# Reordering the start of a fused convolution, SoLU and layer-norm kernel on one Trainium2 core

## The chip, the core and the metric

One core of one Trainium2 chip runs the whole kernel. The engines are TensorE (PE, matmuls; PEld are its weight loads), VectorE (DVE), ScalarE (ACT), GpSimd (POOL) and SyncE (SP), which issues the transfers. The metric is device time in microseconds of one execution, the median of the runs shown. A profile is one further execution; its own clock starts at its first event.

## The reference

`x` is 8 x 4160 x 192. Each of 8 heads (24 columns) has a causal filter of 7 taps, the softmax of its row of `weight`; the result is a matrix of 33,280 rows and 192 columns. Then a layer of 1,024 features:

```python
h = x @ w_in                                  # 192 -> 1024
e = np.exp(h - h_max)                         # h_max: maximum of the row
sm = e / (np.sum(e, axis=-1, keepdims=True) + 1e-09)
solu = h * sm
mu = np.mean(solu, axis=-1, keepdims=True)
var = np.mean((solu - mu) ** 2, axis=-1, keepdims=True)
ln = (solu - mu) / np.sqrt(var + 1e-06) * g_ln
return (ln @ w_out).astype(np.float32)        # 1024 -> 192
```

`w_in` and `w_out` arrive as 64-bit floats, which the kernel reads as pairs of 32-bit words. All matmuls with weights are done in 16-bit halves: a tensor is scaled by a power of two and split into an upper part (rounded to fp16) and a lower part (what is left).

## The kernel before, in words

Rows are worked in 260 tiles of 128. A chunk of x (`xr`) gives its convolution as matmuls with the taps (`pc`, in chunk 0 `pq` and `pr`), split into uppers and lowers in `y`; transposing transfers turn y into `yT`. For a tile, ten matmuls form the scores `ph` (128x1024) from `yT` and `whi`/`wlo`; VectorE takes the maximum (`emit_max`, L803), ScalarE the exponential and its sum (`emit_exp`, L810), VectorE the product of scores and exponentials with its sum (`emit_mul`, L820). ScalarE casts that to the upper part of `p` (`emit_hi`, L831) and GpSimd forms the remainder (`emit_lo`, L846); transposed, they are multiplied with w_out (`po`, L878). There are three score buffers: tile 3 takes tile 0's, the convolution of the next chunk tile 1's, tile 4 tile 2's, each after that tile's product (`emit_mul`).

The order of instructions on each engine is the order of the code; nothing reorders it. Before the steady loop the kernel prepares what all tiles need. The places that the change touches:

- `root_power` (L100 to L113): from a sum of squares a power of two, in four VectorE steps on 128x1 that work on the bits. It gives `s` (scale of chunk 0 of x, from `c0.scale_steps`, L192), `t_in` (w_in, L635) and `t_out` (w_out, L697).
- `sum_squares` (L174): partial sums of squares of x on ScalarE, added up by a matmul (`pt_x`).
- The class `Words` (from L436) rebuilds a weight from its two words: `exponents` (L456) and `mantissas` (L461) mask the high word on VectorE, `lows` scales the low word on GpSimd (L467), `floats` turns the mantissa into a float on ScalarE (L473), `whole` adds both on GpSimd (L484), `join` does the last three at once on VectorE (L490), `powers` forms the power of two on ScalarE (L496), `signs` adds the sign on VectorE (L499), `value` multiplies mantissa and power (L506), `squares` sums the squares on ScalarE (L479). w_in goes through in three parts of 128x512 (`halves[0]`, `halves[1]`, `Z`), w_out at once, 128x1536 (`e_out`, `m_out`, `raw_out`, `f_out`).
- With `t_in`, ScalarE writes the uppers `whi` (L638, L650) and VectorE the lowers `wlo` (L653). `cv` holds the factors for the scores.
- w_out's powers are multiplied by g (`gl`) in `out_powers` (eight ScalarE steps, L692), and summed as squares. GpSimd multiplies the mantissas by them (`value`), `out_mean` (L708) takes column means by matmul, and `out_upper`, `out_lower` (L717 to L726) write the halves `ohl`, with `t_out`.
- `first_two` (L1169) and `second_two` (L1196) issue the steps of tiles 0 to 3 among all this.

Loads of the next chunks of x and of g, and the transposes of y, are issued on SP's queue in the order of the code.

## Time and profile before

| | us |
|---|---|
| median of 3 runs | 1154.21 (1152.86 to 1156.37) |
| span of the profiled execution | 1151.2 |
| of it TensorE busy | 1131.2 (98%) |
| VectorE, ScalarE, GpSimd busy | 994.3, 989.2, 891.5 |
| first score matmul of tile 0 | begins at 17.7 |
| first output matmul | begins at 43.1 |

The span runs from the first to the last event of one execution, which has no time of its own beside it. Times below are microseconds from the span's start, so that 43.1 is the point in the program at which the first output is formed. TensorE's granted clock is a share of full speed, 2.4 GHz. A line number belongs to the kernel that the sentence speaks of.

### The profile page before, as it was taken

The numbers are of one execution on the slowest core, as the hardware profiler recorded it, in microseconds if no ns is written. First come the engines' busy times: TensorE is split into PE (matmuls) and PEld (weight loads), VectorE is DVE, ScalarE is ACT, GpSimd is POOL, SyncE is SP. The second block draws the span as 40 slices with busy tenths as digits, with TensorE's granted clock in tenths as the row PEclk, the third lists the DMA queues.
The fourth block names the chain that finished last, engine by engine and source line by source line (L and its number), as shares of the span: only waits on it lengthen the run. The fifth ranks groups of instructions, "written<-read, shape, count | busy, mean of one in ns | idle before, by whom it ended". The sixth has DMA issues, their size and how long they took to land.

```text
span 1151.2 us, 22389 instructions
## 1 busy us (share of the span) xinstructions
PE 1131.2 (98%) x7742; PEld 691.9 (60%) x7742; DVE 994.3 (86%) x2024; ACT 989.2 (86%) x1789; POOL 891.5 (77%) x709
## 2 busy tenths in 40 slices
PE   5999999999999999999999999999999999999998
PEld 3675656665666666656666566666656666566556
DVE  8888898988888898888888888888888887888787
ACT  7888998888888888988889898888888889888885
POOL 3866899978788687888868788687888868855664
PEclk9999999999999999999999999999999999999999
DMA  7999999999999999999999999999999998999987
GB/s 227 186 184 185 202 207 209 214 206 211 201 213 198 195 204 198 216 191 213 197 204 190 207 199 203 196 205 206 193 213 200 193 205 160 178 164 189 187 158 179
DMA packets 727423, 226.95 MB, mean 197 GB/s; under 512 B 651646, under 2 KB 725902, under 8 KB 727310
## 3 DMA queue, kind: packets, MB, share of 16 engines
q1 hardware_dynamic: 727310, 225.53, 101.9%
q8 instruction: 60, 0.98, 0.3%
q14 instruction: 53, 0.43, 0.1%
HBM read 33.00 MB, written 25.56 MB: 51 GB/s over the span
## 4 chain that ended last, share of the span: by engine, by line
PE 86%; POOL 4%; ACT 3%; issue 2%; DVE 2%; DMA 2%; SPq 1%; POOLq 0%; ACTq 0%; DVEq 0%
PE po L878 39%; PE ph L743 35%; PE pc L281 6%; PE ph L772 5%; POOL p L846 2%; ACT sq L835 1%; DMA pT<-p 1%; DMA raw_in<-in_moe_w_in_dram 1%; DVE ph L803 1%; ACT e L810 1%; POOL xs L243 1%; DMA yT<-y 1%; DVE e L820 0%; POOL xr L240 0%; ACT xs L234 0%
## 5 line engine op out<-in xcount | busy, mean ns | idle before, releaser
L846 POOL TENSOR_TENSOR p<-e,p 128x1024 f16<-128x1024 f32 x257 | 547.6, 2135 | 190.1 <-ACT p L831 189.2
L878 PE MATMUL po<-ohl,pT 128*128 128x192 f16 (+1 forms) x4264 | 539.6, 284 | 0.5
L878 PEld LDWEIGHTS <-pT 128*128 128x128 f16 x4264 | 384.4, 98 | 159.7 <-issue 1.7
L743 PE MATMUL ph<-whi,yT 128*128 128x512 f16 x1548 | 419.4, 380 | 1.7 <-DVE e L820 1.5
L803 DVE TENSOR_SCALAR_CACHE_REDUCE ph<-ph,cv 128x1024 f32<-128x1024 f32 x248 | 319.4, 1289 | 88.4 <-PE ph L772 70.2
L810 ACT ACTIVATE e<-ph,sm 128x1024 f32<-128x1024 f32 x260 | 289.1, 1112 | 100.4 <-DVE ph L803 92.9
L820 DVE SCALAR_TENSOR_TENSOR e<-ph,cv,e 128x1024 f32<-128x1024 f32 x248 | 317.1, 1279 | 24.5 <-ACT e L810 24.1
L743 PEld LDWEIGHTS <-yT 128*128 128x128 f16 x2064 | 192.3, 98 | 230.1 <-issue 36.3
L831 ACT CAST p<-e 128x1024 f16<-128x1024 f32 x245 | 254.4, 1039 | 25.7 <-DVE e L820 23.2
L835 ACT ACTIVATE sq<-e 128x1024 f32<-128x1024 f32 x260 | 273.2, 1051 | 0.2
L743 PE MATMUL ph<-wlo,yT 128*128 128x512 f16 x516 | 153.6, 379 | 0.0
L888 DVE TENSOR_REDUCE raw<-po 128x192 f32<-128x384 f32 x247 | 136.9, 554 | 15.5 <-PE po L878 15.1
L243 POOL TENSOR_TENSOR xs<-xr,xs 128x960 f16<-128x960 f32 (+1 forms) x56 | 107.5, 1919 | 1.3
L772 PE MATMUL ph<-wlo,yT 64*128 64x512 f16 x269 | 74.4, 380 | 0.7 <-DVE e L820 0.7
L281 PE MATMUL pc<-xs,taps_hi 128*112 128x240 f16 (+1 forms) x448 | 72.9, 261 | 0.0
L322 DVE SCALAR_TENSOR_TENSOR y<-pc,y 112x432 f16<-112x432 f32 (+5 forms) x140 | 72.3, 533 | 0.5 <-ACT y L313 0.4
L313 ACT ACTIVATE y<-pc 112x432 f16<-112x432 f32 (+5 forms) x140 | 62.6, 468 | 11.2 <-PE pc L281 5.3
L772 PE MATMUL ph<-wlo,y 64*128 64x512 f16 x251 | 69.0, 380 | 0.0
L181 DVE TENSOR_REDUCE xa<-xr 128x1 f32<-128x384 f32 x112 | 66.7, 618 | 0.0
L281 PEld LDWEIGHTS <-taps_hi 128*112 128x112 f16 x448 | 52.4, 130 | 16.0
L240 POOL TENSOR_SCALAR xr<-xr,s 128x960 f32<-128x960 f32 (+1 forms) x56 | 57.4, 1025 | 3.3 <-ACT xs L234 0.4
L281 PE MATMUL pc<-xs,taps_lo 128*112 128x240 f16 (+1 forms) x224 | 58.5, 261 | 0.0
(150 smaller groups left out, 781.7 us busy)
## 6 DMA issues: line engine op xcount, KB each, us to landing
out_dram<-raw SPq DMA_DIRECT2D x127, 192.0 KB, 2.9
xr<-in_x_dram SPq DMA_DIRECT2D x41, 480.0 KB, 4.9
xr<-in_x_dram SPq DMA_DIRECT2D x22, 384.0 KB, 4.2
pT<-p SPq DMA_TRANSPOSE x263, 4.6
y<-yT SPq DMA_DIRECT2D x15, 140.0 KB, 3.0
y<-yT SPq DMA_DIRECT2D x15, 126.0 KB, 2.7
yT<-y SPq DMA_TRANSPOSE x102, 3.6
raw_out<-in_moe_w_out_dram SPq DMA_DIRECT2D x1, 1536.0 KB, 10.3
```

Of the source, the lines that this page charges most:

```text
L243: (2.1 * size + 0.2, lambda: pool.tensor_tensor(xl, r, h, ALU.subtract)),
L281: nc.tensor.matmul(o, tp[:, h + j, :], r, start=q == 0, stop=q == len(ops) - 1)
L743: nc.tensor.matmul(bank, lhs, w[:, r, n * 512 : (n + 1) * 512], start=start and j == 0, stop=stop and j == len(ops) - 1,)
L772: nc.tensor.matmul(banks_of(t)[n], y[q, t.off : t.off + P], wlo[q, 1, n * 512 : (n + 1) * 512], start=start, stop=not start,)
L803: dve.tensor_scalar(t.ph, t.ph, t.cv[:, 0:1], None, ALU.mult, ALU.min, accum_out=t.bias)
L810: act.activation(t.e, t.ph, AF.Exp, bias=t.bias, scale=-1.0, accum_out=grp.z[:, g : g + 1])
L820: dve.scalar_tensor_tensor(t.e, t.ph, t.cv[:, 3:4], t.e, ALU.mult, ALU.mult, accum_out=t.grp.s1[:, t.g : t.g + 1],)
L831: act.copy(t.p16[:, :, 0, :], t.halves)
L835: act.activation(junk, t.e, AF.Square, accum_out=t.grp.s2[:, t.g : t.g + 1])
L846: eng.tensor_tensor(t.p16[:, :, 1, :], t.halves, t.p16[:, :, 0, :], ALU.subtract)
L878: nc.tensor.matmul(t.po[:, 0:n], t.pT[:, a, :], w, start=j == 0, stop=j == len(ops) - 1)
L888: dve.tensor_reduce(t.grp.raw[:, t.g, :], t.po[:, 0 : 2 * D].rearrange("p (a d) -> p d a", a=2), AX.X, ALU.add,)
```

## The change

1. `root_bits` takes the place of `root_power` for the first `s`, for `t_in` and in `out_scale`: a multiply and a power of -1/2 on GpSimd, then one mask on VectorE (`t_out`'s multiply stays on VectorE).
2. The last 128x576 sum of squares of chunk 0 is done on VectorE; the matmul that adds up the sums comes after all but the last of the first convolution's matmuls.
3. The uppers and lowers of y's first three pieces are written between the steps of w_in's parts; w_in's third part starts later in VectorE's order.
4. g is loaded right behind w_out's words.
5. g is multiplied into w_out's lows (GpSimd, eight steps) and floats (ScalarE, eight steps); `out_powers` is gone.
6. Two of the last four uppers of w_in are written by GpSimd (`upper_twin`).
7. w_out's masks stand ahead of the last lowers of w_in; its signs behind tile 0's product; its powers ahead of tile 0's exponential; the last pieces of y behind tile 1's product.
8. The squares of w_out are summed from the finished floats `f_out` (`out_squares`), behind tile 3's exponential.

```diff
+    def root_bits(dst, src, num, tiny):
+        bits = dst.bitcast(I32)
+        return [
+            lambda: pool.tensor_scalar(dst, src, tiny, 1.0 / num, ALU.max, ALU.mult),
+            lambda: pool.tensor_tensor(dst, dst, mhalf, ALU.pow),
+            lambda: dve.tensor_scalar(bits, bits, EXPO, None, ALU.bitwise_and),
+        ]
...
+            if vector:
+                junk = sp.tile([P, F], F32, name=f"xv_{self.ch}_{col}", tag="e", bufs=4)
+                r = self.raw[j][:, a:z, :]
+                dve.scalar_tensor_tensor(
+                    junk[:, 0 : (z - a) * D].rearrange("p (w d) -> p w d", d=D),
+                    r, 1.0, r, ALU.mult, ALU.mult, accum_out=self.part[:, col : col + 1],
+                )
+                return
...
+    nc.sync.dma_start(gl, g_ln.rearrange("(c p) -> p c", p=P))
...
-        def lows(self, c, scale):
+        def lows(self, c, scale, by):
...
-        def floats(self, c):
-            act.copy(self.m[:, c].bitcast(F32), self.m[:, c])
+        def floats(self, c, by):
+            act.activation(
+                self.m[:, c].bitcast(F32), self.m[:, c], AF.Copy, scale=by
+            )
...
+    def upper_twin(to, of, q):
+        pool.tensor_scalar(to, of, t_in[q], 1.0, ALU.mult, ALU.mult)
...
+    chain0[1]()
+    wi.mantissas(halves[1])
+    for f in chain0[2:4]:
+        f()
+    wi.join(halves[1])
+    chain0[4]()
+    wi.squares(halves[1], isq[:, 1:2])
+    steps[0][0]()
+    wi.signs(halves[1], wi.m)
+    wi.exponents(Z)
+    wi.powers(Z)
+    wi.value(halves[1], wi.m, pool)
+    wi.mantissas(Z)
+    steps[1][0]()
+    wi.squares(Z, isq[:, 2:3])
+    wi.join(Z)
+    steps[2][0]()
+    steps[0][1]()
...
+    wi.signs(Z, wi.m)
+    dve.tensor_reduce(isq[:, 0:1], tp, AX.X, ALU.add)
+    settle_in = root_bits(t_in, isq[:, 0:1], 2.0**26, 1e-12)
+    for f in settle_in[:2]:
+        f()
+    steps[1][1]()
+    settle_in[2]()
...
+    upper_twin(whi[top, 1, 0:HF], wf[top, Z], top)
+    upper_in(whi[low, 1, 0:HF], wf[top, Z], top)
+    upper_twin(whi[low, 1, HF:F], wf[low, Z], low)
+    upper_in(whi[top, 1, HF:F], wf[low, Z], low)
+    wo.exponents(W)
+    wo.mantissas(W)
...
+    for j, c in enumerate(eighths):
+        wo.lows(c, 2.0**-32, gl[:, j : j + 1])
+    for j, c in enumerate(eighths):
+        wo.floats(c, gl[:, j : j + 1])
...
+    def out_squares():
+        junk = sp.tile([P, F], F32, name="oj_out", tag="sq", bufs=1)
+        act.activation(
+            junk.bitcast(F16)[:, 0 : NFC * D], wo.f, AF.Square, accum_out=osq
+        )
...
     first_two:
         emit_max(t)
+        wo.powers(W)
         emit_exp(t)
-        wo.mantissas(W)
-        wo.floats(W)
         wo.whole(W)
-        wo.signs(W, wo.e)
-        emit_mul(t)
-        out_powers()
         emit_max(u)
         emit_exp(u)
-        wo.squares(W, osq)
+        emit_mul(t)
+        wo.signs(W, wo.e)
+        emit_mul(u)
+        for pc, hg in got0:
+            c0.upper(pc, *hg)
         emit_hi(t)
         settle_rest()
-        emit_mul(u)
         emit_hi(u)
...
     second_two:
-        scale = out_scale()
         emit_max(t)
         emit_exp(t)
         out_mean()
         emit_max(u)
         emit_exp(u)
-        emit_square(tiles[0])
+        out_squares()
+        scale = out_scale()
         for f in scale:
             f()
+        emit_square(tiles[0])
         numerators(t)
```

The order on two engines, at three places. VectorE around w_in's third part (`e_in`, `m_in`, `f_in` are the exponent, mantissa and value; `xm` the sum of x, `isq` that of w_in), before:

```order
L456 TENSOR_SCALAR e_in<-raw_in 128x512
L461 TENSOR_SCALAR m_in<-raw_in 128x512
L203 TENSOR_REDUCE xm_170<-pt_x_178 128x1
L105 TENSOR_SCALAR s_171<-xm_170 128x1
L106 TENSOR_SCALAR s_171<-s_171 128x1
L109 TENSOR_SCALAR s_171<-s_171 128x1
L112 TENSOR_SCALAR s_171<-s_171 128x1
L499 SCALAR_TENSOR_TENSOR m_in<-raw_in,e_in 128x512
L490 SCALAR_TENSOR_TENSOR f_in<-raw_in,m_in 128x512
L634 TENSOR_REDUCE isq<-pt_wi 128x1
L105 TENSOR_SCALAR t_in<-isq 128x1
L106 TENSOR_SCALAR t_in<-t_in 128x1
```

and now:

```order
L514 SCALAR_TENSOR_TENSOR f_in<-raw_in,m_in 128x512
L121 TENSOR_SCALAR s_168<-s_168 128x1
L523 SCALAR_TENSOR_TENSOR m_in<-raw_in,e_in 128x512
L478 TENSOR_SCALAR e_in<-raw_in 128x512
L483 TENSOR_SCALAR m_in<-raw_in 128x512
L514 SCALAR_TENSOR_TENSOR f_in<-raw_in,m_in 128x512
L654 SCALAR_TENSOR_TENSOR y_0_0_191<-pq,s_168,y_0_0_191 112x5x96
L523 SCALAR_TENSOR_TENSOR m_in<-raw_in,e_in 128x512
L687 TENSOR_REDUCE isq<-pt_wi 128x1
L654 SCALAR_TENSOR_TENSOR y_0_0_191<-pq,s_168,y_0_0_191 112x5x32
L121 TENSOR_SCALAR t_in<-t_in 128x1
L654 SCALAR_TENSOR_TENSOR y_0_0_191<-pq,s_168,y_0_0_191 112x5x64
```

The masks of the third part (the last `e_in`, `m_in`) stood before the reduction to `xm`; they now stand behind `s` and the signs of the second part, and the pieces of y (`y_0_0`) between the steps up to `t_in`.

ScalarE from w_in's last uppers to tile 1's exponential and on (`e_298`, `e_315` before and `e_309`, `e_314` now are the exponentials of tiles 0 and 1), before:

```order
L650 ACTIVATE whi<-f_in,t_in 64x512 x4
L313 ACTIVATE y_0_0_198<-pr_207,s_171 112x5x96
L313 ACTIVATE y_0_0_198<-pr_208,s_171 112x5x32
L313 ACTIVATE y_0_0_198<-pr_208,s_171 112x5x64
L496 ACTIVATE e_out<-e_out,rebias 128x1536
L810 ACTIVATE e_298,z_269<-ph_274,sm_296 128x1024
L473 CAST m_out<-m_out 128x1536
L692 ACTIVATE e_out<-e_out,gl 128x192 x8
L810 ACTIVATE e_315,z_269<-ph_275,sm_313 128x1024
L479 ACTIVATE oj_out_317,osq<-e_out 128x1536
```

and now:

```order
L495 ACTIVATE m_out<-m_out,gl 128x192 x8
L520 ACTIVATE e_out<-e_out,rebias 128x1536
L870 ACTIVATE e_309,z_279<-ph_284,sm_306 128x1024
L870 ACTIVATE e_314,z_279<-ph_285,sm_312 128x1024
L333 ACTIVATE y_0_0_191<-pr_208,s_168 112x5x96
L333 ACTIVATE y_0_0_191<-pr_209,s_168 112x5x32
L333 ACTIVATE y_0_0_191<-pr_209,s_168 112x5x64
L891 CAST p_0_322<-e_309 128x2x512
L891 CAST p_1_331<-e_314 128x2x512
L870 ACTIVATE e_380,z_279<-ph_347,sm_378 128x1024
L870 ACTIVATE e_393,z_279<-ph_358,sm_391 128x1024
L745 ACTIVATE oj_out,osq<-f_out 128x1536
```

The cast of `m_out` and the eight multiplications of `e_out` by `gl` stood behind tile 0's exponential; eight steps on `m_out` and the powers of `e_out` now stand ahead of it, and the squares of w_out (`oj_out`) have left this stretch for the place behind tile 3's exponential.

VectorE from tile 0's maximum to tile 2's product (`e_298` and `e_380` before, `e_309` and `e_380` now), before:

```order
L803 TENSOR_SCALAR ph_274,sm_296<-ph_274,cv_172 128x1024
L461 TENSOR_SCALAR m_out<-raw_out 128x1536
L499 SCALAR_TENSOR_TENSOR e_out<-raw_out,e_out 128x1536
L820 SCALAR_TENSOR_TENSOR e_298,s_0_270<-ph_274,cv_172,e_298 128x1024
L803 TENSOR_SCALAR ph_275,sm_313<-ph_275,cv_172 128x1024
L322 SCALAR_TENSOR_TENSOR y_0_0_198<-pr_207,s_171,y_0_0_198 112x5x96
L322 SCALAR_TENSOR_TENSOR y_0_0_198<-pr_208,s_171,y_0_0_198 112x5x32
L322 SCALAR_TENSOR_TENSOR y_0_0_198<-pr_208,s_171,y_0_0_198 112x5x64
L820 SCALAR_TENSOR_TENSOR e_315,s_0_270<-ph_275,cv_172,e_315 128x1024
L803 TENSOR_SCALAR ph_345,sm_378<-ph_345,cv_172 128x1024
L803 TENSOR_SCALAR ph_356,sm_391<-ph_356,cv_172 128x1024
L105 TENSOR_SCALAR t_out<-pt_wo 128x1
```

and now, from tile 1's maximum:

```order
L863 TENSOR_SCALAR ph_285,sm_312<-ph_285,cv_169 128x1024
L880 SCALAR_TENSOR_TENSOR e_309,s_0_280<-ph_284,cv_169,e_309 128x1024
L523 SCALAR_TENSOR_TENSOR e_out<-raw_out,e_out 128x1536
L880 SCALAR_TENSOR_TENSOR e_314,s_0_280<-ph_285,cv_169,e_314 128x1024
L342 SCALAR_TENSOR_TENSOR y_0_0_191<-pr_208,s_168,y_0_0_191 112x5x96
L342 SCALAR_TENSOR_TENSOR y_0_0_191<-pr_209,s_168,y_0_0_191 112x5x32
L342 SCALAR_TENSOR_TENSOR y_0_0_191<-pr_209,s_168,y_0_0_191 112x5x64
L863 TENSOR_SCALAR ph_347,sm_378<-ph_347,cv_169 128x1024
L863 TENSOR_SCALAR ph_358,sm_391<-ph_358,cv_169 128x1024
L752 TENSOR_SCALAR t_out<-pt_wo 128x1
L756 TENSOR_SCALAR t_out<-t_out 128x1
L880 SCALAR_TENSOR_TENSOR e_380,s_0_280<-ph_347,cv_169,e_380 128x1024
```

`m_out` is gone from here, the signs (`e_out`) come behind tile 0's product, the three pieces of y behind tile 1's, and the steps of `t_out` are two instead of four, still ahead of tile 2's product.

## Rows read from the trace of the kernel before

**Rows 1.** The page of the kernel before: its first line.
```profile
span 1151.2 us, 22389 instructions
```

**Rows 2.** The span cut into stretches: from:to in us, the length, then for each engine its busy time in us (and number of instructions), and at the end the granted clock of TensorE (1.00 is 2.4 GHz), the mean busy share of the DMA queues and GB/s.
```profile
17.70:38.20 20.50, 16.20 (x73) 9.04 (x74) 18.96 (x33) 19.44 (x33) 13.89 (x11) 0.92 0.95 211
38.20:1130.00 1091.80, 1090.51 (x7456) 662.17 (x7455) 947.41 (x1910) 946.30 (x1708) 866.40 (x677) 1.00 1.03 197
```

**Rows 3.** The chain of waits that ended last, from 24 to 48 us, in order of time: start, length in us, and the engine, tile and line ("issue" is time in which the engine waited for nothing that the profile shows).
```profile
30.46 1.72 issue
32.18 2.67 PE pc L281 x16
...
35.09 3.46 PE mean L708 x16
38.54 1.73 PE ph L743 x8
...
43.17 2.09 PE po L878 x24
```

**Rows 4.** VectorE's timeline from 12 to 22 us: start, busy time, engine, line, operation, out<-in, size, count, and in brackets the idle time just before with what ended it.
```profile
12.26 0.43 DVE L456 TENSOR_SCALAR e_in<-raw_in 128x512 int32<-128x512 int32 x1 [0.57 <-DMA raw_in<-in_moe_w_in_dram]
...
12.93 0.16 DVE L203 TENSOR_REDUCE xm<-pt_x 128x1 f32<-128x4 f32 x1
...
13.76 0.68 DVE L499 SCALAR_TENSOR_TENSOR m_in<-raw_in,e_in 128x512 int32<-128x512 int32 x1
...
14.96 0.15 DVE L634 TENSOR_REDUCE isq<-pt_wi 128x1 f32<-128x3 f32 x1
...
15.71 0.15 DVE L112 TENSOR_SCALAR t_in<-t_in 128x1 int32<-128x1 int32 x1
15.78 0.95 DVE L499 SCALAR_TENSOR_TENSOR m_in<-raw_in,e_in 128x512 int32<-128x512 int32 x1
...
18.03 2.84 DVE L653 SCALAR_TENSOR_TENSOR wlo<-f_in,t_in,whi 128x512 f16<-128x512 f32 x4
20.90 0.96 DVE L456 TENSOR_SCALAR e_out<-raw_out 128x1536 int32<-128x1536 int32 x1
```

**Rows 5.** The same view of VectorE from 22.5 to 44 us.
```profile
22.69 1.29 DVE L803 TENSOR_SCALAR_CACHE_REDUCE ph<-ph,cv 128x1024 f32<-128x1024 f32 x1 [0.52 <-PE ph L772]
...
23.90 1.19 DVE L461 TENSOR_SCALAR m_out<-raw_out 128x1536 int32<-128x1536 int32 x1
25.00 1.75 DVE L499 SCALAR_TENSOR_TENSOR e_out<-raw_out,e_out 128x1536 int32<-128x1536 int32 x1
26.66 1.28 DVE L820 SCALAR_TENSOR_TENSOR e<-ph,cv,e 128x1024 f32<-128x1024 f32 x1
...
29.07 1.47 DVE L322 SCALAR_TENSOR_TENSOR y<-pr,s,y 112x480 f16<-112x480 f32 x3
30.79 1.28 DVE L820 SCALAR_TENSOR_TENSOR e<-ph,cv,e 128x1024 f32<-128x1024 f32 x1 [0.25 <-ACT e L810]
...
33.20 1.29 DVE L803 TENSOR_SCALAR_CACHE_REDUCE ph<-ph,cv 128x1024 f32<-128x1024 f32 x1
...
35.12 0.16 DVE L105 TENSOR_SCALAR t_out<-pt_wo 128x1 f32<-128x1 f32 x1 [0.57 <-PE pt_wo L95]
...
35.77 1.28 DVE L820 SCALAR_TENSOR_TENSOR e<-ph,cv,e 128x1024 f32<-128x1024 f32 x1
...
38.66 1.82 DVE L717 SCALAR_TENSOR_TENSOR f_out<-f_out,mean 128x768 f32<-128x768 f32 x2 [0.40 <-PE mean L708]
40.62 1.95 DVE L726 SCALAR_TENSOR_TENSOR ohl<-f_out,t_out,ohl 128x768 f16<-128x768 f32 x2
```

**Rows 6.** The same view of GpSimd from 12 to 40 us.
```profile
14.53 1.65 POOL L506 TENSOR_TENSOR f_in<-f_in,m_in 128x512 f32<-128x512 f32 x1 [11.85 <-DVE m_in L499]
...
22.65 1.61 POOL L467 TENSOR_SCALAR raw_out<-raw_out 128x1536 f32<-128x1536 uint32 x1
26.78 3.54 POOL L484 TENSOR_TENSOR f_out<-m_out,raw_out 128x1536 f32<-128x1536 f32 x1 [2.52 <-issue]
...
30.48 3.58 POOL L506 TENSOR_TENSOR f_out<-f_out,e_out 128x768 f32<-128x768 f32 x2
```

**Rows 7.** The same view of ScalarE from 13 to 39 us.
```profile
18.11 2.94 ACT L650 ACTIVATE whi<-f_in,t_in 64x512 f16<-64x512 f32 x4 [0.87 <-POOL f_in L506]
...
22.32 1.58 ACT L496 ACTIVATE e_out<-e_out,rebias 128x1536 int32<-128x1536 int32 x1
...
25.09 0.19 ACT L810 ACTIVATION_READ_ACCUMULATOR e<-ph,sm 128x1 f32 x1
...
26.79 2.88 ACT L692 ACTIVATE e_out<-e_out,gl 128x192 f32<-128x192 f32 x8
...
30.66 1.47 ACT L479 ACTIVATE oj_out<-e_out 128x1536 f16<-128x1536 f32 x1
```

**Rows 8.** The same view of GpSimd near the end, 1125 to 1130 us: the kernel's own small GpSimd steps, a power (L903) among them.
```profile
1125.38 0.26 POOL L947 TENSOR_SCALAR t<-t 128x3 f32<-128x3 f32 x1
...
1129.29 0.58 POOL L903 TENSOR_TENSOR t<-t,mhalf 128x1 f32<-128x1 f32 x1
```

**Rows 9.** The span cut into stretches again (columns as in Rows 2).
```profile
33.00:36.50 3.50, 3.50 (x18) 3.50 (x17) 2.82 (x9) 3.50 (x7) 3.50 (x3) 0.51 1.00 220
```

**Rows 10.** The microsecond in which g's load runs (columns as in Rows 2).
```profile
25.00:26.00 1.00, 1.00 (x6) 0.34 (x5) 1.00 (x2) 1.00 (x3) 0.00 (x0) 1.00 1.33 171
```

More of the change, by code (lines that the diff above doesn't have):

```diff
@@ L256, in heads, with product @@
             return [(h, n, a, z) for h in range(0, H, n)]
-        def product(self, h, n, a, z, bank=None):
+        def product(self, h, n, a, z, bank=None, midway=None):
             ops, bank_given = [], bank is not None
@@ L280, in product @@
             for q, (_, j, o, tp, r) in enumerate(ops):
+                if midway and q == len(ops) - 1:
+                    midway()
                 nc.tensor.matmul(
@@ L578 @@
         )
-    words(halves[1])
-    for h in c0.halves(1):
-        c0.sum_squares(*h)
+    (ha, hb) = c0.halves(1)
+    c0.sum_squares(*ha)
+    c0.sum_squares(*hb, vector=True)
+    t_in = cp.tile([P, 1], F32, name="t_in")
+    chain0 = c0.scale_steps()
+    wi.exponents(halves[1])
     wi.powers(halves[1])
@@ L594, in split_taps, with convolve @@
             act.copy(of_blocks(to, q, q + 2), got[:, j])
-    t_in = cp.tile([P, 1], F32, name="t_in")
-    chain0 = c0.scale_steps()
     spans0 = list(zip(c0.cuts, c0.cuts[1:]))
     assert len(spans0) == 2 and len(c0.heads(*spans0[1])) == NH
-    def convolve(a, z, banks):
+    def convolve(a, z, banks, midway=None):
         for hg, bank in zip(c0.heads(a, z), banks):
-            yield c0.product(*hg, bank=bank), hg
+            yield c0.product(*hg, bank=bank, midway=midway), hg
+            midway = None
@@ new lines, with upper_in, lower_in, pieces @@
+    top, low = slice(0, R), slice(R, P)
+    wf = wi.f
+    def upper_in(to, of, q):
+        act.activation(to, of, AF.Copy, scale=t_in[q])
+    def upper_twin(to, of, q):
+        pool.tensor_scalar(to, of, t_in[q], 1.0, ALU.mult, ALU.mult)
+    def lower_in(to, of, hi, q=slice(0, P)):
+        dve.scalar_tensor_tensor(to, of, t_in[q], hi, ALU.mult, ALU.subtract)
+    def pieces(pc, h, n, a, z):
+        col, cuts = h * HD, c0.cut(h * HD, n * HD)
+        for e, f in zip(cuts, cuts[1:]):
+            def up(e=e, f=f):
+                act.activation(
+                    c0.at(0, col + e, col + f, a, z), pc[:, :, e:f], AF.Copy,
+                    scale=c0.scale(),
+                )
+            def down(e=e, f=f):
+                dve.scalar_tensor_tensor(
+                    c0.at(1, col + e, col + f, a, z), pc[:, :, e:f], c0.scale(),
+                    c0.at(0, col + e, col + f, a, z), ALU.mult, ALU.subtract,
+                )
+            yield up, down
@@ new lines @@
+    pq = pair(1, "pq")
+    got1 = list(convolve(*spans0[0], [pq[:, 0:512], pq[:, 512:F]], c0.add_up))
+    steps = [s for pc, hg in got1 for s in pieces(pc, *hg)]
+    assert len(steps) == 3
+    chain0[1]()
[11 more added lines that the diff above has]
+    wi.mantissas(Z)
@@ new lines @@
+    steps[1][0]()
[3 more added lines that the diff above has]
+    steps[0][1]()
+    c0.open(0, None)
+    wo, W = Words(raw_out, "out"), slice(0, NFC * D)
+    tp = total(isq, "wi")
+    got0 = list(convolve(*spans0[1], [single("pr_0"), single("pr_1")]))
+    wi.signs(Z, wi.m)
[5 more added lines that the diff above has]
+    settle_in[2]()
@@ new lines @@
+    for c in halves:
+        act.activation(whi[:, 0, c], wi.f[:, c], AF.Copy, scale=t_in)
+    steps[2][1]()
+    wi.value(Z, wi.m, pool)
+    for blk in (0, 2, 1):
+        c0.turn(blk, *spans0[0])
+    for j in range(chunks[1].np):
+        chunks[1].load(j)
+    for c in halves:
+        lower_in(wlo[:, 0, c], wf[:, c], whi[:, 0, c])
+    upper_twin(whi[top, 1, 0:HF], wf[top, Z], top)
+    upper_in(whi[low, 1, 0:HF], wf[top, Z], top)
+    upper_twin(whi[low, 1, HF:F], wf[low, Z], low)
+    upper_in(whi[top, 1, HF:F], wf[low, Z], low)
@@ new lines @@
+    wo.exponents(W)
+    wo.mantissas(W)
+    lower_in(wlo[top, 1, 0:HF], wf[top, Z], whi[top, 1, 0:HF], top)
+    lower_in(wlo[top, 1, HF:F], wf[low, Z], whi[low, 1, HF:F], low)
+    for c in chunks[2:3]:
+        for j in range(c.np):
+            c.load(j)
+    for f in chain0[-3:]:
+        f()
+    sums1 = [h for j in range(chunks[1].np) for h in chunks[1].halves(j)]
+    eighths = [slice(j * D, (j + 1) * D) for j in range(NFC)]
+    for j, c in enumerate(eighths):
+        wo.lows(c, 2.0**-32, gl[:, j : j + 1])
```

80 lines of the change are left out of this document (14 added, 66 removed).

## The prediction

> **What bounds the kernel now.** I read the page, then the span cut into stretches, then the chain of waits over the prologue's end, then each engine's timeline there. The span is 1151.2 us [rows 1]; the median is 3.0 us above it, so I work out a shift of the span's own events and add it to the median, 1154.21. From 38.20 to 1130.00 TensorE works 1090.51 of 1091.80 us [rows 2]: it is the bound there, with nothing to win or lose, and the instructions of that part are the same in both kernels. The change touches only what comes earlier, and whatever moves the first output matmul, 43.17 [rows 3], moves the end by as much. The reader is to see that in the stretch from 17.70 to 38.20 TensorE idles 4.3 of 20.50 us [rows 2], and is never idle once it has begun the sums of the next x at 32.18 [rows 3]. From there the chain runs through the column means (35.09, 3.46 us) and tiles 4 and 5 to the first output, which also needs w_out's two halves, finished by VectorE at 40.62 + 1.95 = 42.57 [rows 5].
>
> **What releases TensorE.** Three score buffers exist. Tile 3's matmuls wait for tile 0's product with the exponentials (mul0, which ends at 27.94), the next x for mul1 (32.07), tile 4 for mul2 (37.05) [rows 5], though in the kernel before tile 4 starts only when the means are through, at 38.54 [rows 3]. So I follow mul0, mul1 and mul2.
>
> **Who delays whom on SBUF.** One effect has to be priced first. m_in's combining step takes 0.68 us at 13.76 and 0.95 at 15.78 [rows 4]; in the second case GpSimd's product runs from 14.53 to 16.18 [rows 6], and VectorE ends 0.55 after it. m_out's mask takes 1.19 at 23.90 [rows 5], with GpSimd's pass over raw_out until 24.26 [rows 6], and ends 0.83 after that. GpSimd's own product at 14.53 takes 1.65 us. So wide VectorE steps on SBUF and wide GpSimd steps take turns: who comes second starts when the first ends. VectorE steps on 128x1 at 14.96 to 15.86 [rows 4] and those that read PSUM, as mul0 under the 3.54 us sum at 26.78 [rows 5, 6], are not held up. Whether a 128x1 GpSimd step waits for a wide VectorE step is in no row: it costs from 0 to 0.69 us, one wide step; I take 0.5, nearer to the wait, since the wide steps above show one in both directions. The Trainium skill (SBUF — State Buffer, Who interferes with whom) says that a VectorE instruction with two SBUF inputs and a GpSimd one that reads SBUF lock each other out for the whole instruction, whatever their size; by it a small GpSimd step would wait out the whole 0.69, and the sum would be 0.2 higher. The wide steps above agree with it (0.55 and 0.83 after GpSimd's end); no row here shows a small one.
>
> **The change, part by part.**
>
> *x's scale.* The sum over the last 128x576 moves from ScalarE to VectorE, about 0.77 us (0.68 x 576/512 [rows 4]), in time in which VectorE waited for w_in's last load: 0.57 idle before 12.26 [rows 4]. The column sum no longer stands behind the third part's masks (12.93 [rows 4]). The power itself gets longer: four steps of 0.15 us are replaced by 0.26 and 0.55 on GpSimd [rows 8], 0.15 on VectorE and two hand-overs. With 0.5 of waiting behind VectorE's joining step s is ready at about 12.75, 1.0 before 13.76, where VectorE's next step begins now [rows 4]; y's pieces use that, and behind its mask VectorE's signs are queued, so this wait is on the path.
>
> *w_in's scale, t_in.* The third part's exponent mask now stands behind the signs of the part before: 13.3 for 12.26. Its mantissa mask meets GpSimd's product of the second part, 13.45 to 15.0, and ends at 15.3. Then come the joining and the signs (0.69 each, as 13.76 [rows 4]), a piece of y between them (0.71, half of the three [rows 5]) and the reduction: 17.3, for 15.11 before. GpSimd's two steps and VectorE's mask take 1.2 where four small ones took 0.75 (15.11 to 15.86 [rows 4]). t_in: 18.5, **2.6 later** (without turns 16.75, 0.9 later).
>
> *w_in's halves.* ScalarE's first upper takes about 0.73 us, as each of the four further ones (2.94 together [rows 7]), to 19.2. Two of those four go to GpSimd, about 0.55 each (1.61 x 512/1536 [rows 6]), and take turns with VectorE's lowers (2.84 for four [rows 4]). VectorE now does w_out's exponents and mantissas, 0.96 each (20.90 [rows 4]), ahead of the last two lowers. With some 0.6 us of turns it is done at 24.6, and the first maximum starts at 25.06 instead of 22.69 [rows 5].
>
> *w_out's floats and powers before the first exponential.* m_out is there at 23.3. ScalarE then turns it into floats times g in eight steps, priced as the eight scalings of 2.88 us that they replace [rows 7], to 26.2, and only then takes the powers, 1.58 us [rows 7]: 27.65. So the first exponential waits 1.2 us more for its engine than for its maximum (26.4), and ends at 28.8, **3.5 later** than 25.28 (25.09 + 0.19 [rows 7]). mul0 ends at 30.1 for 27.94 (before, VectorE came to it only after the signs, at 26.66 [rows 5]). Tile 3's matmuls: **+2.1**.
>
> *w_out's signs.* They now follow mul0, while GpSimd adds floats and lows, which I put at 27.7 to 31.2 (the lows in eight parts take about 2.1 from the cv step at 25.0, then 3.54 [rows 6]). The 1.75 us step [rows 5] begins at 31.2 in effect and ends at 32.9; mul1 ends at 34.1 for 32.07: the sums of x **+2.0**. Tile 3's matmuls are through by then, so TensorE idles.
>
> *Pieces of y.* The last three lowers (1.47 [rows 5]) stood ahead of mul1 where 0.25 us was idle; now they stand behind it and ahead of the maxima of tiles 2 and 3, which end at 38.1 for 34.49 [rows 5]: **+3.5**. y's second transposes are issued at 35.6, about 5 us later, and are wanted by tile 4, at 43.35 below.
>
> *w_out's squares.* They were done on the powers at 30.66 (1.47 us [rows 7]), long before t_out's first step at 35.12 [rows 5]. Now ScalarE does them on the finished floats after tile 3's exponential: 39.3, then 1.5 to 40.8, TensorE's column sum to 41.1, and t_out's steps with GpSimd's power to 42.1. On VectorE these steps stand **ahead of mul2**, which needs none of them. So mul2 ends at 43.3 for 37.05, and tile 4 starts at 43.35 for 38.54 [rows 3]. The means are no longer the limit (through by about 40.2: GpSimd's values end at 36.5, and 3.46 [rows 3] follow), nor is GpSimd's queue: the two remainders of p that follow are over at 40.7.
>
> *First output.* From mul2's end at 37.05 to w_out's last half it took 5.5 us, the wait for the means among it; now mul3, two differences and two lower halves (1.28 + 1.82 + 1.95 [rows 5]) take 5.05: 48.4. Tiles 4 and 5 need 4.6 us: 48.0. First output 48.4, against 43.17 [rows 3]: **+5.3**.
>
> *Clock.* After two idle stretches the granted clock fell to 0.51 between 33.00 and 36.50 [rows 9], so 1.2 GHz where the rest has 2.4. At half rate 3.5 us hold 1.75 us of work. The new idle time ends at 43.35, later and longer; a like stretch would then lie on tiles 4 and 5, of which 0.4 us is covered by w_out's halves: 0 to +1.3. I take **+0.7**.
>
> *Costed at nothing.* g's load of 1,024 floats moves ahead of x's and y's transfers; in the microsecond in which it now runs the queues move 171 GB/s [rows 10] against a mean of 211 [rows 2], under half a microsecond of transfers, and the first transposed y is wanted later than before. On SP's queue it is one issue behind raw_out's. g in GpSimd's lows replaces one 1.61 us step [rows 6] by eight smaller ones: 0.5 more, under ScalarE's powers. If that cover goes, the sum on GpSimd and then the signs are 0.5 later.
>
> **Sum:** 5.3 + 0.7 = +6.0 us, so 1154.21 + 6.0 = 1160.2.
>
> **Rivals.**
> *No turns.* If those two long steps had another cause, t_in comes at 16.75, mul0 ends at 27.5, mul1 at 30.4, the maxima at 34.4, the squares at 37.1 and mul2 at 39.6. w_out is whole at 44.7 and the first output comes 1.6 later, with the clock up to 2.9: about 1156.3. For it: two rows only show turns. Against it: both end a full step after GpSimd.
> *Not slower.* If tile 3's maximum were over by about 33, then exponential (1.3), squares (1.7), column sum, t_out (1.3) and mul2 (1.3) end at 38.5, the wait for t_out costs nothing, and tile 4 starts with the means' end. Without turns GpSimd's values end at 32.85, the means at 36.5 instead of 38.5: 2.0 less, 1152.2. It decides at 33; I work out 38.1, and 34.4 without turns.
> *More idle, more half clock.* The whole 1.75 us falls on the path, or the low clock lasts longer, and GpSimd's small steps wait 0.7 each: 1162.5 and above.
>
> **How the numbers follow.** Forecast 0.57 (its own range 1158.7 to 1161.5: the small waits and the clock at either end), no turns 0.25, not slower 0.08, more half clock 0.10. Range 1154.5 to 1162.5 leaves the last two out, 0.18. A measurement of this kernel tells about 0.3%, 3.5 us: no turns lies within that, 1152.2 too, but for 0.05 in which more of the idle time is won; slower 0.66, same 0.29, faster 0.05.
>
> **What would show it.** Right: t_in's last step at 18 to 19; long masks or signs on VectorE where GpSimd's products run; the first exponential ending near 28.8; VectorE idle between tile 3's maximum and t_out, some 3 us, released by TensorE's column sum, with mul2 behind; a low granted clock after it; first output near 48. Wrong: mul2 right behind the maxima; w_out's signs in 1.75 us under GpSimd's sum; a first output before 45; or a difference that arises after 50 us.

## The result, and the profile after

The changed kernel takes 1159.85 us (median of 4 runs, 1158.74 to 1161.52) against 1154.47 for the kernel before (4 runs, 1152.86 to 1156.37): **5.4 us slower**, ratio 1.0053, 95% interval 1.0040 to 1.0066 (4.6 to 7.6 us). 1160.2 was predicted.

The span of the profiled execution is 1157.0 us, 5.8 more than before [rows 1]. First the page's line, then the stretches that answer to [rows 2] (columns as there), cut where the prologue ends here, and the stretch of tiles 4 and 5:

```profile
span 1157.0 us, 22396 instructions
```

```profile
17.70:43.50 25.80, 20.41 (x82) 11.49 (x82) 20.19 (x30) 17.21 (x29) 20.34 (x23) 0.82 0.60 156
43.50:1136.00 1092.50, 1089.27 (x7451) 662.05 (x7452) 949.11 (x1913) 947.31 (x1712) 866.45 (x677) 1.00 1.03 197
...
45.40:50.20 4.80, 4.76 (x21) 1.67 (x22) 4.66 (x6) 2.77 (x5) 1.03 (x1) 1.00 1.23 225
```

TensorE now idles 5.4 of 25.8 us in the prologue's second half (4.3 of the same stretch before), at a mean granted clock of 0.82 (0.93 before). After it it is busy to 0.3%, and most of that is the end of the wait up to 45.44: the loss arises before the first output. The chain of waits there, which answers to [rows 3]:

```profile
41.18 1.47 ACT oj_out L745 x2
42.65 0.04 issue
42.70 0.40 PE pt_wo L95 x2
43.09 0.02 issue
43.12 0.17 DVE t_out L752
43.29 0.07 issue
43.35 0.56 POOL t_out L755
43.92 0.02 issue
43.94 0.15 DVE t_out L756
44.09 1.21 DVE e L880 x2
45.30 0.14 issue
45.44 1.89 PE ph L803 x8
...
50.23 2.09 PE po L938 x24
```

Where before the column means released tile 4, it is now the sum of w_out's squares, t_out's three steps and tile 2's product, one behind the other, as the prediction had it. First output at 50.23 for 43.17. VectorE's timeline, which answers to [rows 4, 5]:

```profile
14.26 1.49 DVE L483 TENSOR_SCALAR m_in<-raw_in 128x512 int32<-128x512 int32 x1
...
18.86 0.15 DVE L121 TENSOR_SCALAR t_in<-t_in 128x1 int32<-128x1 int32 x1 [0.73 <-POOL t_in L120]
...
22.50 1.37 DVE L483 TENSOR_SCALAR m_out<-raw_out 128x1536 int32<-128x1536 int32 x1
...
25.88 1.29 DVE L863 TENSOR_SCALAR_CACHE_REDUCE ph<-ph,cv 128x1024 f32<-128x1024 f32 x1
...
29.49 1.28 DVE L880 SCALAR_TENSOR_TENSOR e<-ph,cv,e 128x1024 f32<-128x1024 f32 x1 [0.84 <-ACT e L870]
...
30.70 4.20 DVE L523 SCALAR_TENSOR_TENSOR e_out<-raw_out,e_out 128x1536 int32<-128x1536 int32 x1
34.82 1.27 DVE L880 SCALAR_TENSOR_TENSOR e<-ph,cv,e 128x1024 f32<-128x1024 f32 x1
...
38.60 1.28 DVE L863 TENSOR_SCALAR_CACHE_REDUCE ph<-ph,cv 128x1024 f32<-128x1024 f32 x1
...
43.12 0.16 DVE L752 TENSOR_SCALAR t_out<-pt_wo 128x1 f32<-128x1 f32 x1 [3.17 <-PE pt_wo L95]
...
44.01 1.27 DVE L880 SCALAR_TENSOR_TENSOR e<-ph,cv,e 128x1024 f32<-128x1024 f32 x1
...
48.37 1.95 DVE L786 SCALAR_TENSOR_TENSOR ohl<-f_out,t_out,ohl 128x768 f16<-128x768 f32 x2
```

and GpSimd's, which answers to [rows 6]:

```profile
12.23 0.97 POOL L120 TENSOR_TENSOR s<-s,mhalf 128x1 f32<-128x1 f32 x1
14.09 1.38 POOL L530 TENSOR_TENSOR f_in<-f_in,m_in 128x512 f32<-128x512 f32 x1 [0.89 <-DVE m_in L523]
...
18.25 0.57 POOL L120 TENSOR_TENSOR t_in<-t_in,mhalf 128x1 f32<-128x1 f32 x1
...
20.16 2.90 POOL L639 TENSOR_SCALAR whi<-f_in,t_in 64x512 f16<-64x512 f32 x2
...
26.32 3.34 POOL L489 TENSOR_SCALAR raw_out<-raw_out,gl 128x192 f32<-128x192 uint32 x8
29.74 3.54 POOL L508 TENSOR_TENSOR f_out<-m_out,raw_out 128x1536 f32<-128x1536 f32 x1
```

To be seen, line against line: the mantissa mask of w_in's third part takes 1.49 us (its other instances 0.42) and ends 0.28 after GpSimd's product; w_out's signs take 4.20 for 1.75 [rows 5] and end 1.62 after GpSimd's sum; GpSimd's two uppers take 2.90 together beside VectorE's lowers and masks. And ScalarE's, which answers to [rows 7]: the powers come after the floats and right ahead of tile 0's exponential, the squares late.

```profile
23.96 2.87 ACT L495 ACTIVATE m_out<-m_out,gl 128x192 f32<-128x192 int32 x8 [2.09 <-issue]
26.73 1.56 ACT L520 ACTIVATE e_out<-e_out,rebias 128x1536 int32<-128x1536 int32 x1
...
29.19 0.19 ACT L870 ACTIVATION_READ_ACCUMULATOR e<-ph,sm 128x1 f32 x1
...
41.08 1.47 ACT L745 ACTIVATE oj_out<-f_out 128x1536 f16<-128x1536 f32 x1
```

**A caution on reading these times against each other.** Below, the first output is counted from the start of VectorE's second exponent mask on w_in ("counted"): 43.10 - 10.19 = 32.91 before, 50.16 - 10.89 = 39.27 after, 6.4 us more. With the start of the kernel before, that mask waits for w_in's second load, which ended at 10.2 to 12.3 us in the profiles of this case, and differently for the same code ahead of it. So one execution's event stands up to 2 us from another's with no edit as a cause.

The count is rough, too. With the new start the column sum of x, from which s comes, begins 4.7 us after w_in's first mask (6.88 and 11.55 in the changed kernel), or 4.9 in the one run where the second load held it up. In three of those runs (new start only, t_out behind, three edits) the second mask waits for no load but stands right behind VectorE's new sum of squares. Counted from the first mask (6.45 before), the changed kernel is 6.6 us later, and the runs with its start come out from 0.1 lower to 0.8 higher than in the table. Of the 7.06 us between the two profiles 0.4 to 0.7 is thus the loads, and differences under 1 us between single profiles carry little.

### The profile page after: what moved, and what is told of

Its sections match the earlier page's. It is cut to its first block, busy times and chain, and to the rows that moved or that the text cites. A ratio compares the mean times of both kernels' runs of the same rounds, so it can differ in the third digit from the quotient of the medians.

```text
span 1157.0 us, 22396 instructions
## 1 busy us (share of the span) xinstructions
PE 1134.4 (98%) x7742; PEld 693.9 (60%) x7742; DVE 997.9 (86%) x2018; ACT 985.9 (85%) x1784; POOL 898.5 (78%) x723
## 4 chain that ended last, share of the span: by engine, by line
PE 91%; ACT 2%; issue 2%; DVE 2%; POOL 1%; DMA 1%; SPq 0%; POOLq 0%; DVEq 0%; ACTq 0%
PE po L938 42%; PE ph L803 38%; PE pc L301 6%; PE ph L832 6%; DVE e L880 1%; ACT e L870 1%; ACT sq L895 0%; DMA xr<-in_x_dram 0%; DMA raw_in<-in_moe_w_in_dram 0%; POOL p L906 0%; DVE ph L863 0%; ACT m_out L495 0%; POOL p L889 0%; SPq L908 0%; PE pc L95 0%
```

## The experiments

All times are ratios to runs of the kernel before on the same chip.

| run | w_in's second mask begins | first output | counted, to before | ratio (95%) |
|---|---|---|---|---|
| before | 10.19 | 43.10 | 0 | 1 |
| after | 10.89 | 50.16 | +6.4 | 1.0053 (1.0040 to 1.0066) |
| new start only | 10.34 | 44.55 | +1.3 | 1.0011 (1.0002 to 1.0021) |
| new w_out only | 10.47 | 47.82 | +4.4 | 1.0044 (1.0029 to 1.0059) |
| t_out behind | 10.92 | 49.44 | +5.6 | 1.0050 (1.0031 to 1.0069) |
| signs early | 10.87 | 50.70 | +6.9 | 1.0063 (1.0043 to 1.0082) |
| no turns | 11.97 | 51.60 | +6.7 | 1.0057 (1.0042 to 1.0072) |
| three edits | 10.52 | 45.52 | +2.1 | 1.0007 (0.9998 to 1.0016) |
| three edits, no turns | 11.76 | 45.15 | +0.5 | 1.0009 (0.9999 to 1.0018) |
| three edits, old start | 10.81 | 43.14 | -0.6 | 0.9995 (0.9984 to 1.0005) |
| powers on GpSimd only | 12.25 | 45.08 | -0.1 | 1.0004 (0.9995 to 1.0014) |
| g early only | 11.83 | 44.79 | +0.1 | 0.9997 (0.9988 to 1.0006) |
| TensorE kept busy | 11.19 | 44.41 | +0.3 | 0.9993 (0.9984 to 1.0002) |
| ... and x's loads later | 12.03 | 43.36 | -1.6 | 0.9996 (0.9987 to 1.0005) |

0.001 of the ratio is 1.15 us. Counted shift and ratio agree within 0.7 us, but for 1.1 to 1.3 in the run with three edits and the last two.

**The two halves of the change.** The first kernel has points 1 to 4 and 6 of the change (without t_out's part of point 1) with w_out built as before, the second points 5, 7 and 8 and t_out's part with the old start; both load g early.

> The new start alone (scales on GpSimd, the sum of x on VectorE, y between w_in's steps, g loaded early, the two uppers on GpSimd), with w_out built as in the kernel before. Theory (the start loses on turns of VectorE and GpSimd and on the longer chain to w_in's scale, w_out's build on its late powers, signs and squares): t_in at 19.0 as in the changed kernel, tile 0's product ends 2.3 later than before (30.2), the first output begins at about 45.6 for 43.2, time +2.4 us against the kernel before. Rival (the whole loss is the wait for t_out ahead of tile 2's product): first output at 43.2 to 43.7, time within 0.5 us of before, since the squares are taken early here.

> The start as in the kernel before, w_out built as in the changed kernel (g in lows and floats, powers ahead of the first exponential, signs behind tile 0's product, squares from the finished floats), g loaded early. Theory: t_in at 15.9 as before, first exponential ends at about 26.9, tile 1's product ends at 33.5 (32.1 before), tile 2's at 42.8 (37.1 before), first output at about 47.7 for 43.2, time +4.5 us; together with the start alone about the sum that the changed kernel shows (7.1 at the first output). Rival (the wait for t_out is only the late start's consequence): with the old start the squares come in time, tile 2's product ends by 38, time within 1 us of before.

Measured +1.3 and +4.4 at the first output, 1.0011 and 1.0044. Together 5.7 of the 6.4. Both rivals fall, the first by less: the new start alone makes the first output 1.3 later without any late squares, though the interval of its time begins at 0.2 us, inside the rival's 0.5. W_out's new build has the same signs and the same wait ahead of tile 2's product with the old start. VectorE in the second:

```profile
28.35 4.20 DVE L502 SCALAR_TENSOR_TENSOR e_out<-raw_out,e_out 128x1536 int32<-128x1536 int32 x1
...
40.77 0.16 DVE L701 TENSOR_SCALAR t_out<-pt_wo 128x1 f32<-128x1 f32 x1 [3.17 <-PE pt_wo L95]
```

The start cost 1 us less than expected (1.3 for 2.4). In its profile the sums of the next x and the means took 1.87 and 2.85 us, where the kernel before took 2.67 and 3.60: the half clock lay ahead of them, on tile 3's scores (granted clock 0.50 from 32 to 34 us), which were through at 34.72, just as tile 1's product ended (34.69), for which the sums wait in any case. Whether the late start moved it there is not shown (see the clock runs below).

**t_out behind tile 3's product.**

```diff
-        for f in scale:
-            f()
         emit_square(tiles[0])
         numerators(t)
         c.sum_squares(*sums1[0])
         emit_mul(u)
+        for f in scale:
+            f()
```

> The changed kernel with t_out's three steps moved behind tile 3's product on VectorE (and the ScalarE step that stood behind them in the code unchanged in its engine's order). Theory: VectorE's idle 3.2 + 0.7 us ahead of tile 2's product is gone, that product ends at 41.2 instead of 45.3; tile 4 then starts behind the means and the column sum of w_out's squares, at 43.1 instead of 45.4; first output at 47.9 instead of 50.2, time 2.3 us below the changed kernel (about +3.6 against before). Rival (w_out's halves are the limit of the first output anyway): tile 4 earlier, first output no more than 0.5 us earlier.

Tile 4 started at 43.42 instead of 45.44, as expected. But the first output came only 0.8 earlier (+5.6 for +6.4; 1.2 counted from the first mask), more than 1 us short of the theory. TensorE:

```profile
49.44 2.15 PE L938 MATMUL po<-ohl,pT 128*128 128x192 f16 x24 [1.24 <-DMA pT<-p]
```

The next wait stood right behind: not w_out's halves (at 48.82), which the rival named, but the transposes of tile 0's `p`, whose remainder GpSimd forms only after w_out's values. Since those wait for the late signs, the wait for t_out covered a second delay of nearly the same size.

**Signs ahead of GpSimd's sum.**

```diff
+    wo.powers(W)
     for j, c in enumerate(eighths):
         wo.floats(c, gl[:, j : j + 1])
...
+        wo.signs(W, wo.e)
         emit_max(t)
-        wo.powers(W)
         emit_exp(t)
...
         emit_mul(t)
-        wo.signs(W, wo.e)
         emit_mul(u)
```

> The changed kernel with w_out's powers ahead of its floats on ScalarE and w_out's signs ahead of tile 0's maximum on VectorE, before GpSimd begins its long sum. Theory (turns): the signs take 1.75 us instead of 4.20, the first exponential 0.8 later, tile 1's product ends 3.3 us earlier (32.8 for 36.1), GpSimd's lows begin 1.2 later; tile 2's product then waits for the means and the sum behind them: it ends 1 us earlier, 44.2, and the first output at 49.1, time 1 us below the changed kernel. Rival (the signs were long for a reason of their own, not for GpSimd's sum): 4 us again, now ahead of the first maximum, time 3 us above the changed kernel.

The signs took 1.75 us at 25.50, and tile 1's product ended at 32.35 for 36.09: 3.74 earlier. So the 4.20 us was GpSimd's turn. The time did not fall (1.0063). t_out on VectorE and GpSimd, then TensorE:

```profile
40.48 0.16 DVE L753 TENSOR_SCALAR t_out<-pt_wo 128x1 f32<-128x1 f32 x1 [4.28 <-PE pt_wo L95]
43.12 0.15 DVE L757 TENSOR_SCALAR t_out<-t_out 128x1 int32<-128x1 int32 x1 [2.48 <-POOL t_out L756]
```

```profile
44.62 1.01 PE L804 MATMUL ph<-whi,yT 128*128 128x512 f16 x2 [4.18 <-DVE e L881]
```

t_out's power now stood behind two remainders of p on GpSimd (38.36 to 42.57), so mul2 gained 0.8 us; and after 4.18 us of idle time tile 4 ran at half clock (2 matmuls in 1.01 us, 0.59 at full), which took that away and more. My expectation had only the means as the next wait: missed.

**No wide GpSimd step beside VectorE's masks in the start.**

```diff
-    wi.value(halves[1], wi.m, pool)
+    wi.value(halves[1], wi.m, dve)
-    upper_twin(whi[top, 1, 0:HF], wf[top, Z], top)
+    upper_in(whi[top, 1, 0:HF], wf[top, Z], top)
-    upper_twin(whi[low, 1, HF:F], wf[low, Z], low)
+    upper_in(whi[low, 1, HF:F], wf[low, Z], low)
```

> The changed kernel with the second part's value on VectorE and the two uppers back on ScalarE, so that GpSimd runs nothing wide beside VectorE's masks up to w_out's. Theory (turns): the third part's mantissa mask takes 0.42 us instead of 1.49 (but the value adds 0.69 to VectorE), w_in's first lowers 1.5 instead of 1.9 and m_out 0.96 instead of 1.37; the first maximum ends at 26.2 instead of 27.2, the first exponential 0.8 earlier, the first output at 49.3 instead of 50.2, time 0.9 us below the changed kernel. Rival (GpSimd's two uppers take load off ScalarE, on the path): the floats of w_out begin later than 24.0, first exponential later, time no lower.

The masks shrank as expected:

```profile
15.88 0.42 DVE L483 TENSOR_SCALAR m_in<-raw_in 128x512 int32<-128x512 int32 x1
...
23.08 0.95 DVE L483 TENSOR_SCALAR m_out<-raw_out 128x1536 int32<-128x1536 int32 x1
```

Counted so, the first exponential came 0.8 and tile 4 0.9 us earlier than in the changed kernel (45.58 - 11.97 against 45.44 - 10.89). The time was the same. In the profiled execution tiles 4 and 5 met the low clock, which took the 0.9 back; for the other executions there is no profile. The chain has tile 4's first eight matmuls at 3.19 us, for 1.89 above:

```profile
45.58 3.19 PE ph L803 x8
```

**The three edits together** (signs early; t_out behind; its power by `root_power` on VectorE), then with no turns as well, then with the old start.

```diff
     def out_scale():
-        bits, tp = t_out.bitcast(I32), total(osq, "wo")
-        return [...]
+        return root_power(t_out, total(osq, "wo"), 2.0**26, 1e-30)
```

> The changed kernel with three edits: powers and signs of w_out early (as in the run with early signs), t_out's power by VectorE's four small steps, and these behind tile 3's product. Theory (signs' turn with GpSimd's sum, then t_out behind GpSimd's remainders, then t_out ahead of tile 2's product, one behind the other): tile 2's product ends at 37.5 instead of 45.3, tile 4 starts behind means and column sum at 40.4, the first remainder's transposes are issued at 40.5 and land at 45.3, w_out's lower halves end at 45.2, first output at 45.3 to 46.5 instead of 50.2, time about +2.6 us against before. Rival (one of these alone is the cause and the others only its cover): no better than the run with t_out behind, first output at 49.

> The three edits of the run before it together with no turns in the start (second part's value on VectorE, the two uppers on ScalarE). Theory: another 0.9 us, first output at about 44.8, time +1.7 against before. Rival (the first output now waits for the transposes of p behind x's loads, which do not come sooner): same as the three edits alone.

> The start of the kernel before with w_out built as in the changed kernel and the same three edits. Theory: t_in at 15.9, signs at 23.3 to 25.1, the first maximum at 26.3, tile 0's product 28.9, tile 2's 35.8, GpSimd's values 35.5 (34.1 before), means 39.0, first output at about 43.9 for 43.2, time +0.8 against before, within what the runs can tell. Rival (g in lows and floats costs more than it saves in any order): first output after 45.

Counted +2.1, +0.5 and -0.6; expected +2.1 to 3.3, +1.7 and +0.8 by absolute times. The three edits, two of which alone gained 0.8 and lost 0.5, take back 4.3 of the 6.4 us: the delays lay behind one another. The third, t_out's power on VectorE, was not run alone. Between the second and the third of these runs is what is left of the new start; that this is the longer chain to t_in is argued, not shown. The last is level with the kernel before (0.9995, 0.9984 to 1.0005), and 1.0053 against 0.9995 puts it clearly below the changed kernel. By ratio the second was no lower than the first (1.0009 and 1.0007), and of the 1.6 us between them 0.7 is left when both are counted from the first mask: that this edit helps here is not shown. GpSimd in the last settles a price that the trace before had in no row:

```profile
23.50 2.23 POOL L208 TENSOR_SCALAR cv<-cv 128x1 f32<-128x1 f32 x3 [4.87 <-DVE cv L205]
```

Three steps on 128x1, 0.61 us together in the kernel before, took 2.23: VectorE's signs ran from 23.51 to 25.26. In the run with early signs, where they ran beside these steps as well, it was 2.16. Small GpSimd steps do wait for a wide VectorE step.

**Powers on GpSimd alone, and g early alone.** Each is the kernel before with one edit: `root_bits` for the first s and t_in; the load of `gl` behind w_out's words.

```diff
-                *root_power(self.s, self.all, 2.0**30, 1e-14),
+                *(root_power if ch else root_bits)(self.s, self.all, 2.0**30, 1e-14),
...
-    for f in root_power(t_in, isq[:, 0:1], 2.0**26, 1e-12):
+    for f in root_bits(t_in, isq[:, 0:1], 2.0**26, 1e-12):
```

```diff
+    nc.sync.dma_start(gl, g_ln.rearrange("(c p) -> p c", p=P))
...
     for j in range(chunks[1].np):
         chunks[1].load(j)
-    nc.sync.dma_start(gl, g_ln.rearrange("(c p) -> p c", p=P))
```

> The kernel before with nothing changed but the powers for the first s and for t_in, which go to GpSimd (two steps) and one VectorE mask. Theory (the power on GpSimd is the longer chain, and it stands in a queue): s 0.4 later (14.2), GpSimd's product of w_in's second part then runs to about 16.5 and t_in's two steps stand behind it, so t_in at 17.4 for 15.9; tile 0's product and the first output 1.5 later, time +1.5 us against before. Rival (two steps are as good as four, since VectorE has other work): t_in at 16.2 or sooner, time within 0.4.

> The kernel before with g's load alone moved ahead, behind w_out's words. Theory (hidden): x's and w_in's loads land where they did, to the spread of single executions (the first of w_in 6.3 to 7.9 in the profiles so far), first transposed y at 17.7 or sooner, first output within 0.3 us, time the same to 0.1%. Rival (g's small packets delay what is loaded beside them): the second load of x and w_in's second part land 0.6 us later in every execution, time +0.6.

g's load shows no cost (0.9997, 0.9988 to 1.0006; counted +0.1). The loads landed late in that run, as in the one with the powers, which loads g at its old place: so not by g. The powers made t_in 1.5 later, counted, for the reason given, as GpSimd shows:

```profile
16.75 1.65 POOL L515 TENSOR_TENSOR f_in<-f_in,m_in 128x512 f32<-128x512 f32 x1 [0.88 <-DVE m_in L508]
18.38 0.24 POOL L119 TENSOR_SCALAR t_in<-isq 128x1 f32<-128x1 f32 x1
```

Yet the first output was not later, and the time 1.0004 (0.9995 to 1.0014): the +1.5 (1.0013) is just inside. TensorE ran the sums of x and the means at full clock in that execution, where [rows 3] has 2.67 and 3.46:

```profile
35.56 1.86 PE L290 MATMUL pc<-xr,taps 128*112 128x120 f32 x16 [1.73 <-issue]
...
37.41 2.85 PE L717 MATMUL mean<-f_out,even 128*128 128x192 f32 x16
```

That is 1.4 us less. But the late start is not shown as its cause. In the run with g early, TensorE idled as long ahead of tile 3 and ahead of the sums (1.51 and 1.73 us in both), and the clock was low:

```profile
33.87 2.57 PE L281 MATMUL pc<-xr,taps 128*112 128x120 f32 x16 [1.73 <-issue]
...
36.53 3.70 PE L708 MATMUL mean<-f_out,even 128*128 128x192 f32 x16
```

So the length of the idle time does not decide it alone, and nothing here tells what else does.

**TensorE kept busy.** The kernel before with its two idle stretches filled by repeated matmuls (`again` is (7, 8) for tiles 2 and 3); then with x's next loads, which stood ahead of the values, behind the first transposes of p.

```diff
         for slot, q, more in ((2, t, again[0]), (0, u, again[1])):
             q.ph = pair(slot, f"ph_{q.i}")
+            for j in range(more):
+                nc.tensor.matmul(
+                    banks_of(q)[j % NH], q.yT[:, 0, q.off : q.off + P],
+                    whi[:, 0, j % NH * 512 : (j % NH + 1) * 512],
+                    start=True, stop=True,
+                )
```

> The kernel before, with TensorE kept busy in its two idle stretches: tile 2's first matmul is repeated 7 times and tile 3's 8 times ahead of the real ones, into the same score buffers (work without use). Theory (the low clock at the sums of x and the means follows the idle time): granted clock 1.00 there, the 16 matmuls of the sums take 1.9 us instead of 2.7 and those of the means 2.9 instead of 3.6, tile 4 starts 1.2 us earlier counted from w_in's second load, and the first output 0.75 earlier, because the transposes of p then end last; time 0.75 us below before, at the edge of what the runs tell. Rival (the low clock has another cause, or the means wait for GpSimd's values anyway): same lengths as before, time the same.

```profile
33.54 1.90 PE L281 MATMUL pc<-xr,taps 128*112 128x120 f32 x16
...
35.42 2.85 PE L708 MATMUL mean<-f_out,even 128*128 128x192 f32 x16
...
44.41 2.15 PE L884 MATMUL po<-ohl,pT 128*128 128x192 f16 x24 [1.52 <-DMA pT<-p]
```

Full clock, as the theory has it; but the run with the powers had it with the idle time left in, so this does not show that the filling brought it. Tile 4 starts 1.3 us earlier, counted (38.10 - 11.19 against 38.38 - 10.19). The first output did not: it waited 1.5 us for p's transposes.

```diff
-        for c in chunks[3:4]:
-            for j in range(XR - sum(q.np for q in chunks[1:3])):
-                c.load(j)
         for c in out_halves:
             wo.value(c, wo.e, pool)
         for q in (t, u):
             emit_lo(q, pool)
+        for c in chunks[3:4]:
+            for j in range(XR - sum(q.np for q in chunks[1:3])):
+                c.load(j)
```

> The run before it (the kernel before with TensorE kept busy in its two idle stretches) with the next two loads of x issued behind the first two transposes of p instead of ahead of them. Theory (those transposes stand behind x's loads in the queues): the first lands about 4.5 us after its issue instead of 6.7, TensorE's 1.5 us of idle time ahead of the first output is gone, the first output comes 1.2 us earlier than before counted from w_in's second load, time 1.2 us below before, the lowest of all. Rival (the transposes take their time by themselves, or x is then late for a later chunk): landing as before, or TensorE idle before 100 us, time no lower than the run before it.

That wait was gone: first output 1.6 us earlier, counted. But TensorE then waited 0.63 us for the third tile's transposes:

```profile
52.92 2.15 PE L884 MATMUL po<-ohl,pT 128*128 128x192 f16 x24 [0.63 <-DMA pT<-p]
```

By ratio (0.9993 and 0.9996) neither can be told from the kernel before. No kernel here is shown to beat it.

## Why the prediction was right, step by step

**The mechanism held at each step.** Forecast and found, in the profile's own times: t_in 18.5 and 19.0; the first maximum's start 25.1 and 25.9; the first exponential's end 28.8 and 29.4; mul0 30.1 and 30.8; mul1 34.1 and 36.1; tile 3's maximum 38.1 and 39.9; the squares 40.8 and 42.6; mul2 43.3 and 45.3; first output 48.4 and 50.2. Of each difference 0.4 to 0.7 is the later loads. Up to mul0 no more than 0.4 is left beside them.

**One term was mis-sized.** From mul1 on everything is 1.1 to 1.6 us later still, and most of it arises in one place: GpSimd's lows in eight parts, priced at 2.1 us, took 3.34 (0.42 each, where 1.61 us for the whole [rows 6] gives 0.2). The sum on GpSimd ended at 33.3 instead of 31.2, the signs behind it at 34.9 instead of 32.9. The note that eight steps cost "0.5 more" was the same error. A step on 128x1 takes 0.2 us (cv's three 0.61); with an eighth of what 1.61 leaves beyond that, an estimate for one part is 0.38, so most of the excess is the cost of each further step. No run separates it from the factor g that each part takes. GpSimd's two uppers were also put at 0.55 each and took 1.45 with their turns; beside them VectorE's first lowers took 1.91 for 1.48 and m_out's mask 1.37 for 0.95 (the short ones in the run without turns), 0.85 us of turns where 0.6 was put. In the sum itself, 48.4 less 43.17 is 5.2, not 5.3.

**The clock term fell elsewhere.** +0.7 was taken for a half clock on tiles 4 and 5. In the changed kernel's profile these ran at 1.00 (the row 45.40:50.20 above), in two of the experiments at half clock, at 1.3 to 1.4 us. So the bounds 0 to 1.3 held to 0.1, and for this kernel's profiled execution the value was 0. The reason given, that the low clock follows the idle time, is not borne out as it stands: the same two idle stretches were followed by the low clock in the kernel before and with g early, and by full clock with the powers on GpSimd. With lows +1.2 and clock -0.7 the sum of 6.0 would have become 6.5, against 6.4 counted; the runs' medians say 5.4, within the interval of 4.6 to 7.6. That 1160.2 lies 0.35 from the measured median is therefore partly luck: the lows were put 1.2 too low, and the clock 0.7 too high.

**The turns are shown**, not only argued: the signs took 4.20 us behind GpSimd's sum and 1.75 without it, m_in's mask 1.49 and 0.42, m_out's 1.37 and 0.95. The rule quoted from the Trainium skill (SBUF — State Buffer, Who interferes with whom) is borne out for small steps too: s's power took 0.97 us beside VectorE's joining step and t_in's 0.57 alone, and cv's three took 2.23 for 0.61. That rule is of VectorE steps with two SBUF inputs. The masks have one, so m_out's in the prediction (0.83) was no example of it; that they wait as well is shown by their lengths. I had put s's wait at 0.5; it was 0.4 (0.97 for 0.57), and 0.1 in the multiply ahead of it (0.34 for t_in's 0.24).

**The rivals.** "No turns" is refuted by the signs and the masks above. "Not slower" needed tile 3's maximum over by 33; it ended at 39.9. "More half clock" did not happen in the profiled run. What the forecast did not see is that the wait for t_out hid two others, GpSimd's remainders with the transposes of p, and GpSimd's queue ahead of t_out's power; they changed nothing in the total but decide what mending one part is worth.

**What stays open.** How often the low clock falls on tiles 4 and 5 of the changed kernel can't be said from one profile each. Of the 0.7 us by which the counted parts fall short of their sum (1.3 + 4.4 for 6.4), no run tells the source. Between the first output and the last output matmuls the two profiles drift 0.6 us towards each other, and 0.7 more behind them; that is one execution each. Nor is the granted clock the whole account of TensorE's speed: with the powers on GpSimd the second convolution ran at half the rate of the kernel before (1.87 us for the same 16 matmuls), in a stretch, 16.4 to 20.0 us, whose granted clock is given as 1.00; why is open.

```profile
16.47 3.52 PE L290 MATMUL pr<-xr,taps 128*112 128x120 f32 x16
```
